# Block means of v from pair sums: three averaging products per batch instead of six

## The chip, the cores and the metric

The kernel runs on one core of one Trainium2 chip. Its time is the device time of one launch in microseconds (us), the median of 3 runs: 488.06 us, with runs from 487.51 to 488.13 us. Engines are named as in the profile: PE (TensorE, with PEld for its weight loads), DVE (VectorE), ACT (ScalarE), POOL (GpSimd) and SP (SyncE, which issues all DMAs here; SPq is its queue).

## The reference

Three layers follow each other. The first is an attention of 2 batches, 8 heads, 768 tokens and 64 features per head, in which each token sees the tokens fewer than 16 positions away and, beside them, 24 block summaries (a block is 32 tokens). The second and third are feed-forward layers over the 1536 tokens, 512 wide. Only this part of the attention touches the change:

```python
k_sum = k.reshape(B, H, nb, block, D).max(axis=3)
v_sum = v.reshape(B, H, nb, block, D).mean(axis=3)        # block = 32, nb = 24
...
v_all = np.concatenate([v, v_sum], axis=2)
return np.matmul(a, v_all)
```

So per batch 24 rows of 512 values are wanted, each the mean of 32 neighbouring rows of v.

## The kernel before, in words

Everything is float32. PE takes a float32 product with 128x512 outputs as two passes; the feed-forward products use pairs of a rounded high part and a rest ("hi" and "lo"), three products each (`mm3x`, lines 104 to 106).

**Block means (`sum_v`, line 180 on).** Six DMAs bring 128 tokens each into `v_sb`. For each, one PE product with a slice of the matrix `avg` as stationary operand adds the means of its four blocks to 24 rows of `vs_ps`: `avg` holds 1/32 at row r, column 120 + r // 32, and the slice that starts at column 24 - 4i puts the blocks of the i-th 128 tokens into their rows. ACT copies the 24 rows to `vsum`, and POOL copies them below the windows of v (`vw`, line 97), where the attention's second product (`x_ps`, line 251) reads them. `sum_v(0)` runs at the start, `sum_v(1)` at the first tick of the main loop. The tile of `v_sb` for batch 1 gives its buffer on to `k_sb` of batch 1 (line 168), so that load waits until the products on `v_sb` are done. The four `ksum` maxima of DVE (line 173) read that `k_sb`.

**What runs beside it.** Attention of 64 tokens at a time is cut in three: scores (`s_ps`, line 215; masks on DVE, line 221; exponentials on ACT, line 224; normalising on POOL, line 229), transposes (`p_ps`, line 234, and the copy `pT`, line 236) and the product with v (`x_ps`). Two such pieces give an `xT` tile of 128 tokens, a hi part by ACT (line 135) and a lo part by DVE (line 101), which the products `h` with `w_in` read. The weights arrive as 64-bit words and are converted: ACT line 122, POOL line 125, DVE lines 126, 127 and 131, then ACT line 135 for hi and DVE line 101 for lo. Eight such conversions, of `w_in`, run in the first 50 us.

**Who sets the order.** Through the first two layers the program's own order holds on SP (a manual schedule), so every DMA stands where the code issues it. On the other engines a scheduler that times the program in advance orders the instructions; an edit at one place can therefore move instructions far from it. (In the later part of the third layer PE's order is the program's own too.) Each engine runs its list strictly in that order.

Of the kernel before, what the change touches and what calls it, by code (L numbers as in the profile page):

```python
# [15 lines left out]
ALU = mybir.AluOpType  # L16
# [3 lines left out]
B, H, S, D = 2, 8, 768, 64  # L20
BLOCK, WINDOW = 32, 16
NB = S // BLOCK
# [4 lines left out]
PAD = 16  # L27
NP = H // 2
DM, F1, F2 = 512, 1024, 2048
# [22 lines left out]
def tile_kernel(ctx: ExitStack, tc: tile.TileContext, qd, kT, v, w_in, w_out, g_ln, w_in2, w_out2,  # L52
                ident_d, mask_d, avg_d, out):
    nc = tc.nc
# [38 lines left out]
    avg = p_at.tile([128, 128 + NB], F32, name="avg", bufs=1)  # L93
# [84 lines left out]
    def sum_v(b):  # L178
        pst = psb.tile([128, DM], F32, tag="b", name="vs_ps")
        v_sb = p_k.tile([128, NP, S + 2 * PAD], F32, tag="k", name="v_sb", bufs=2).rearrange("p a s -> p (a s)")  # L180
        for i in range(S // 128):
            vt = v_sb[:, i * DM:(i + 1) * DM]
            nc.sync.dma_start(vt, v[b, PAD + i * 128:PAD + (i + 1) * 128, :])
            c0 = NB - i * 4
            nc.tensor.matmul(pst, lhsT=avg[:, c0:c0 + 128], rhs=vt, start=i == 0, stop=i == S // 128 - 1)
        vsum[b] = p_at.tile([128, DM], F32, tag="vsum", name="vsum", bufs=1)
        nc.scalar.activation(vsum[b][WIN:KW, :], pst[WIN:KW, :], AF.Copy)

# [14 lines left out]
    def attn_s(n):  # L203
        b, t = divmod(n, NT)
        j, half = divmod(n, 2)
        kw = kws[n % NKW]
        if n not in q_bd:
            load_q(n)
        if t < NKW and n:
            copy_pool(kw[:, :, WIN:KW], ksum[b])  # L210
        if n < NCOPY:
            copy_pool(kw[:, :, 0:WIN], k_sb[b][:, :, t * TQ:t * TQ + WIN])
        sps = psb.tile([128, NP, 128], F32, tag="b", name="s_ps")
        for p in range(NP):
            nc.tensor.matmul(sps[:, p, 0:KW], lhsT=q_bd[n][:, p, :], rhs=kw[:, p, :], start=True, stop=True)  # L215
        sm = p_at.tile([128, NP, KW], F32, tag="sm", name="sm", bufs=NBUF)
        st = p_at.tile([128, 4, NP], F32, tag="st", name="st", bufs=NBUF)
        nm, ss, ri = (st[:, i, :] for i in range(3))
        mi = 1 if t == 0 else (2 if t == NT - 1 else 0)
        for p in range(NP):  # L220
            nc.vector.tensor_tensor_reduce(sm[:, p, :], sps[:, p, 0:KW], mask[:, mi, :], -scale, 3.0e38,  # L221
                                           op0=ALU.add, op1=ALU.min, accum_out=nm[:, p:p + 1])
        for p in range(NP):
            nc.scalar.activation(sm[:, p, :], sm[:, p, :], AF.Exp, bias=nm[:, p:p + 1], scale=-1.0,  # L224
                                 accum_out=ss[:, p:p + 1])
        nc.vector.tensor_scalar(ri, ss, 1e-9, None, op0=ALU.add)
        nc.vector.reciprocal(ri, ri)  # L227
        for p in range(NP):
            nc.gpsimd.tensor_scalar(sm[:, p, :], sm[:, p, :], ri[:, p:p + 1], 1.0, op0=ALU.mult, op1=ALU.mult)  # L229
        live[n] = sm  # L230
# [209 lines left out]
    def more(n=1):  # L440
        for _ in range(n):
            if conv:
                conv.pop(0)()
# [23 lines left out]
    nc.sync.dma_start(ident, ident_d)  # L467
    load_q(0)
    more()
    nc.sync.dma_start(avg, avg_d)  # L470
    attn_s(0)
    more()
    attn_s(1)
    sum_v(0)
    more(2)
    attn_p(0)
# [29 lines left out]
    for t, (j, n) in enumerate(ticks):  # L506
        s_n, p_n, x_n = t + LEAD, t + LEAD - 2, t + LEAD - 3
        if t == 0:
            sum_v(1)
        elif t == 1:  # L510
            load_k(1)
        elif t == 3:
            sum_k(1)
# [263 lines left out]
```

## Time and profile before

| | us |
|---|---|
| median of 3 runs (lowest, highest) | 488.06 (487.51, 488.13) |
| the profiled execution | 489.18 |
| its span | 487.4 |
| PE busy | 461.4 (95%) |
| DVE busy | 330.6 (68%) |
| ACT busy | 284.2 (58%) |
| POOL busy | 120.2 (25%) |

The profile is of one execution, whose time is the span and 1.78 us around it. A share of the span is a mean over parts with different limits: in the first 12 us PE does nothing, and in the last 37 us DVE next to nothing. The chain that ended last lies 71% on PE and 14% on DVE. "Idle before" and "waited for" are inferred from semaphores. The ends of PE's products are modelled, so that PE reads as busy where its next product already stands in line.

### The profile page before, as it was taken

To read this page: it belongs to the slowest core of one execution; us is meant where nothing else is said; L and a number is where in the kernel's file an instruction comes from. 1 tells how busy PE (TensorE), PEld (TensorE's weight loads), DVE (VectorE), ACT (ScalarE), POOL (GpSimd) and SP (SyncE) were. 2 spreads that over 40 slices of the span, in tenths; PEclk is the share of its full clock that TensorE was granted. 3 is DMA by queue.
4 is the path that set the end of the run, shared out by engine and by line. 5 is a ranking of instruction groups with operands and counts; after the bars stand their busy time and mean duration, and the time that the engine had idled before them with its cause. 6 is when DMAs were issued, how large, how long until landed. Compare 5 with 4: busy or idle time off the path is not lost.

```text
span 487.4 us, 7395 instructions
## 1 busy us (share of the span) xinstructions
PE 461.4 (95%) x2568; PEld 389.2 (80%) x2568; DVE 330.6 (68%) x747; ACT 284.2 (58%) x623; POOL 120.2 (25%) x198
## 2 busy tenths in 40 slices
PE   0989999899998999999999999999999999999996
PEld 0666688689997998899888778888888888888885
DVE  3699869988489377969898999567665565541000
ACT  1675788786568347654864757457676666660001
POOL 2797375475425221312212200000000000000000
PEclk9989999999999999999999999999999999999999
DMA  8994668555253413397679754551112212278112
GB/s 280 359 349 153 181 183 287 173 172 180 68 165 121 150 60 103 110 327 242 210 245 305 270 194 152 184 205 44 64 67 87 86 44 86 94 303 292 47 43 86
DMA packets 40117, 82.47 MB, mean 169 GB/s; under 512 B 9616, under 2 KB 18448, under 8 KB 40080
## 3 DMA queue, kind: packets, MB, share of 16 engines
q1 hardware_dynamic: 40080, 82.00, 50.5%
q8 instruction: 20, 0.33, 0.3%
q14 instruction: 17, 0.14, 0.1%
HBM read 70.46 MB, written 11.53 MB: 168 GB/s over the span
## 4 chain that ended last, share of the span: by engine, by line
PE 71%; DVE 14%; DMA 6%; ACT 3%; issue 3%; POOL 2%; SPq 0%; ACTq 0%; DVEq 0%; POOLq 0%
PE o_ps L106 8%; PE o_ps L104 7%; PE o_ps L105 7%; PE c L104 5%; PE c L105 5%; PE c L106 5%; PE h L106 5%; PE h L104 5%; PE h L105 5%; PE y_ps L104 4%; PE y_ps L106 4%; PE y_ps L105 4%; PE s_ps L215 3%; DVE conv L127 2%; ACT sm L224 2%
## 5 line engine op out<-in xcount | busy, mean ns | idle before, releaser
L125 POOL TENSOR_SCALAR conv<-conv 128x512 f32<-128x512 f32 x48 | 38.0, 792 | 93.4 <-ACT conv L122 91.3
L229 POOL TENSOR_SCALAR sm<-sm,st 128x120 f32<-128x120 f32 x96 | 47.1, 508 | 30.8 <-DVE st L227 26.3
L104 PE MATMUL o_ps<-w4r,g_hl 128*128 128x512 f32 x128 | 49.9, 390 | 0.3 <-ACT g_hl L135 0.3
L105 PE MATMUL o_ps<-w4r,g_hl 128*128 128x512 f32 x128 | 49.8, 389 | 0.0
L106 PE MATMUL o_ps<-w4r,g_hl 128*128 128x512 f32 x128 | 45.5, 391 | 0.2 <-DVE g_hl L101 0.2
L104 PE MATMUL y_ps<-lnT,w_out 128*128 128x384 f32 x128 | 43.7, 341 | 1.1 <-DVE lnT L101 1.0
L105 PE MATMUL y_ps<-lnT,w_out 128*128 128x384 f32 x128 | 43.2, 337 | 0.0
L106 PE MATMUL y_ps<-lnT,w_out 128*128 128x384 f32 x128 | 43.0, 337 | 0.0
L104 PE MATMUL h<-w_in,xT 128*128 128x512 f32 x96 | 39.9, 415 | 2.5 <-ACT xT L135 2.5
L215 PE MATMUL s_ps<-kw,q_bd 128*128 128x120 f32 x192 | 28.1, 295 | 13.3 <-POOL kw L97 12.1
L224 ACT ACTIVATE sm<-sm,st 128x120 f32<-128x120 f32 x96 | 36.8, 389 | 5.2 <-DVE st L221 5.2
L106 PE MATMUL h<-w_in,xT 128*128 128x512 f32 x96 | 38.7, 403 | 0.7 <-DVE xT L101 0.7
L215 PEld LDWEIGHTS s_ps<-kw,q_bd 128*128 128x128 f32 x192 | 26.1, 207 | 15.4 <-POOL kw L97 12.1
L105 PE MATMUL h<-w_in,xT 128*128 128x512 f32 x96 | 38.1, 397 | 0.0
L612 DVE COPY y<-o_ps 128x512 f32<-128x512 f32 x5 | 3.4, 690 | 42.9 <-PE o_ps L106 42.9
L584 ACT ACTIVATE y<-y 128x512 f32<-128x512 f32 x48 | 30.0, 627 | 0.8
L614 ACT ACTIVATE y<-o_ps 128x512 f32<-128x512 f32 x6 | 3.6, 598 | 43.9 <-PE o_ps L106 43.9
L104 PEld LDWEIGHTS o_ps<-w4r,g_hl 128*128 128x128 f32 x128 | 24.0, 188 | 5.7 <-ACT g_hl L135 0.7
L106 PEld LDWEIGHTS o_ps<-w4r,g_hl 128*128 128x128 f32 x128 | 23.8, 188 | 5.9 <-DVE g_hl L101 1.1
L122 ACT ACTIVATE conv<-y 128x512 f32<-128x512 f32 x30 | 20.0, 670 | 14.4 <-DMA y<-in_w_in 12.8
L105 PEld LDWEIGHTS o_ps<-w4r,g_hl 128*128 128x128 f32 x128 | 24.1, 188 | 5.0
L101 DVE TENSOR_TENSOR g_hl<-y,g_hl 128x512 fp32r<-128x512 f32 x32 | 22.1, 692 | 8.2 <-ACT g_hl L135 7.9
(146 smaller groups left out, 1254.4 us busy)
## 6 DMA issues: line engine op xcount, KB each, us to landing
w4r<-w4d SPq DMA_DIRECT2D x38, 512.0 KB, 3.8
y<-in_w_in SPq DMA_DIRECT2D x16, 512.0 KB, 5.5
w4d<-w3f SPq DMA_DIRECT2D x16, 512.0 KB, 3.1
y<-in_w_out SPq DMA_DIRECT2D x14, 512.0 KB, 5.4
q_bd<-in_qd SPq DMA_DIRECT2D x24, 256.0 KB, 5.8
bits<-in_w_out SPq DMA_DIRECT2D x10, 512.0 KB, 5.4
w4l<-w4d SPq DMA_DIRECT2D x10, 512.0 KB, 4.2
vw<-in_v SPq DMA_DIRECT2D x24, 192.0 KB, 4.1
```

Of the source, the lines that this page charges most:

```text
L101: nc.vector.tensor_tensor(out_, x, hi.bitcast(F32), op=ALU.subtract)
L104: nc.tensor.matmul(ps, lhsT=l[0][ls], rhs=r[0][rs], start=first, stop=False, skip_group_check=parts)
L105: nc.tensor.matmul(ps, lhsT=l[0][ls], rhs=r[1][rs], start=False, stop=False, skip_group_check=parts)
L106: nc.tensor.matmul(ps, lhsT=l[1][ls], rhs=r[0][rs], start=False, stop=last, skip_group_check=parts)
L122: first = nc.scalar.activation(x, high.bitcast(F32), AF.Abs)
L125: nc.gpsimd.tensor_scalar(x, x, F64_HUGE, F64_TINY, op0=ALU.min, op1=ALU.max)
L127: nc.vector.scalar_tensor_tensor(a, high, -0x40000000, a, op0=ALU.bitwise_and, op1=ALU.bitwise_or)
L215: nc.tensor.matmul(sps[:, p, 0:KW], lhsT=q_bd[n][:, p, :], rhs=kw[:, p, :], start=True, stop=True)
L224: nc.scalar.activation(sm[:, p, :], sm[:, p, :], AF.Exp, bias=nm[:, p:p + 1], scale=-1.0, accum_out=ss[:, p:p + 1])
L229: nc.gpsimd.tensor_scalar(sm[:, p, :], sm[:, p, :], ri[:, p:p + 1], 1.0, op0=ALU.mult, op1=ALU.mult)
L584: nc.scalar.activation(m, m, AF.Exp, scale=-1.0)
L614: nc.scalar.activation(o, ops[t], AF.Copy)
```

## The change

A batch's v is loaded by three DMAs of 256 tokens; a partition receives two neighbouring tokens side by side. DVE adds the second to the first, and one product per DMA averages the sums, three in place of six. A sum of two tokens has its block at row r // 16, so `avg` has to hold 1/32 at column 120 + r // 16. The array in memory stays as it was; two DMAs of 64 rows each fetch its rows in another order: blocks of 16 rows (every second block of 16) fill 64 partitions, the second time shifted by 4 columns. The second leaves columns 0 to 3 of its 64 partitions unwritten; the slices that the products read begin at columns 24, 16 and 8.

```diff
-        for i in range(S // 128):
-            vt = v_sb[:, i * DM:(i + 1) * DM]
-            nc.sync.dma_start(vt, v[b, PAD + i * 128:PAD + (i + 1) * 128, :])
-            c0 = NB - i * 4
-            nc.tensor.matmul(pst, lhsT=avg[:, c0:c0 + 128], rhs=vt, start=i == 0, stop=i == S // 128 - 1)
+        for i in range(S // 256):
+            vt = v_sb[:, i * 2 * DM:(i + 1) * 2 * DM].rearrange("p (r f) -> p r f", r=2)
+            nc.sync.dma_start(vt, v[b, PAD + i * 256:PAD + (i + 1) * 256, :].rearrange("(p r) f -> p r f", r=2))
+            nc.vector.tensor_tensor(vt[:, 0], vt[:, 0], vt[:, 1], op=ALU.add)
+            c0 = NB - i * 8
+            nc.tensor.matmul(pst, lhsT=avg[:, c0:c0 + 128], rhs=vt[:, 0], start=i == 0, stop=i == S // 256 - 1)
...
-    nc.sync.dma_start(avg, avg_d)
+    for h in range(2):
+        nc.sync.dma_start(avg[h * 64:(h + 1) * 64, h * 4:], avg_d.rearrange("(c h p) k -> c h p k", h=2, p=16)[
+            :, 0, :, :128 + NB - h * 4])
```

The scheduler orders PE, DVE, ACT and POOL anew, up to the middle of the second layer. Line numbers behind line 185 grow by one in the changed kernel (226 becomes 227, 227 becomes 228), those behind line 470 by three. Two places on DVE are shown.

First, DVE's list after the masks of the first two pieces, while the first two weight tiles are converted (`conv`, `w_in`) and their softmax sums inverted (`st`). Before:

```order
L126 TENSOR_SCALAR conv<-conv 128x512
L227 RECIPROCAL st<-st 128x4
L127 SCALAR_TENSOR_TENSOR conv<-y_65,conv 128x512
L131 SCALAR_TENSOR_TENSOR conv<-y_65,conv 128x512
L226 TENSOR_SCALAR st<-st 128x4
L227 RECIPROCAL st<-st 128x4
L126 TENSOR_SCALAR conv<-conv 128x512
L101 TENSOR_TENSOR w_in_90<-conv,w_in_89 128x512
L127 SCALAR_TENSOR_TENSOR conv<-y_65,conv 128x512
L131 SCALAR_TENSOR_TENSOR conv<-y_65,conv 128x512
L101 TENSOR_TENSOR w_in_90<-conv,w_in_89 128x512
L126 TENSOR_SCALAR conv<-conv 128x512
```

The same place in the changed kernel:

```order
L126 TENSOR_SCALAR conv<-conv 128x512
L184 TENSOR_TENSOR v_sb<-v_sb 128x512
L228 RECIPROCAL st<-st 128x4
L127 SCALAR_TENSOR_TENSOR conv<-y_65,conv 128x512
L227 TENSOR_SCALAR st<-st 128x4
L184 TENSOR_TENSOR v_sb<-v_sb 128x512
L131 SCALAR_TENSOR_TENSOR conv<-y_65,conv 128x512
L228 RECIPROCAL st<-st 128x4
L126 TENSOR_SCALAR conv<-conv 128x512
L184 TENSOR_TENSOR v_sb<-v_sb 128x512
L127 SCALAR_TENSOR_TENSOR conv<-y_65,conv 128x512
L101 TENSOR_TENSOR w_in_90<-conv,w_in_89 128x512
```

The three additions of batch 0 (L184) stand between the steps of the first two conversions, the first of them ahead of the reciprocal on which POOL's normalising waits.

Second, DVE's list around the lo part of the second `xT` tile (tokens 128 to 255), at the end of the eighth conversion. Before:

```order
L101 TENSOR_TENSOR w_in_90<-conv,w_in_89 128x512
L173 TENSOR_REDUCE ksum<-k_sb 128x24 x2
L226 TENSOR_SCALAR st<-st 128x4
L221 ISA sm,st<-s_ps,mask 128x120
L221 ISA st 128x1
L221 ISA sm,st<-s_ps,mask 128x120
L221 ISA st 128x1
L101 TENSOR_TENSOR xT<-x_ps,xT 128x512
```

The same place in the changed kernel:

```order
L131 SCALAR_TENSOR_TENSOR conv<-y_65,conv 128x512
L227 TENSOR_SCALAR st<-st 128x4
L173 TENSOR_REDUCE ksum<-k_sb 128x24
L228 RECIPROCAL st<-st 128x4
L101 TENSOR_TENSOR xT<-x_ps,xT 128x512
L101 TENSOR_TENSOR w_in_90<-conv,w_in_89 128x512
L173 TENSOR_REDUCE ksum<-k_sb 128x24
```

The `xT` part has moved ahead of the eighth conversion's lo part, of one maximum and of two masks; one maximum still stands ahead of it.

## Rows read from the trace of the kernel before

**Rows 1.** Busy time by stretch: stretch, length, busy us (instructions) per engine, clock, DMA.
```profile
24.00:36.00 12.00, 9.82 (x78) 8.31 (x78) 11.61 (x41) 9.35 (x34) 11.25 (x17) 0.86 0.98 347
36.00:48.00 12.00, 11.45 (x82) 7.60 (x82) 10.94 (x34) 6.74 (x21) 9.95 (x15) 1.00 0.47 153
48.00:60.00 12.00, 11.28 (x87) 9.06 (x86) 10.66 (x33) 8.42 (x27) 3.87 (x11) 1.00 0.63 179
300.00:350.00 50.00, 50.00 (x222) 41.40 (x221) 33.89 (x47) 33.97 (x56) 0.00 (x0) 1.00 0.35 120
```

**Rows 2.** Chain that ended last, in order of time: start us, us, what.
```profile
40.67 0.68 DVE conv L127
41.44 0.93 DVE w_in L101
47.79 1.72 DVE ksum L173 x2
49.98 0.61 DVE xT L101
50.64 0.50 PE h L106
```

**Rows 3.** Timeline of PE: start us, us, engine, line, [idle before <- releaser].
```profile
39.77 2.74 PE L185 MATMUL vs_ps<-v_sb,avg 128*128 128x512 f32 x6
50.64 0.50 PE L106 MATMUL h<-w_in,xT 128*128 128x512 f32 x1 [0.72 <-DVE xT L101]
```

**Rows 4.** Tile vs_ps: duration ns min/median/max, first and last start.
```profile
L185 PE MATMUL vs_ps<-v_sb,avg x24: 592/592/1064, 15.6 to 41.9; 128*128 128x512 f32 x24
```

**Rows 5.** Line 101 from 12 to 52 us: duration ns min/median/max.
```profile
L101 DVE TENSOR_TENSOR w_in<-conv,w_in x8: 692/740/1006, 19.7 to 47.1; 128x512 fp32r<-128x512 f32 x8
```

**Rows 6.** Groups of DVE by form, 12 to 52 us: busy us, mean ns, idle before.
```profile
L221 DVE CUSTOM_DVE_ANT_0 sm<-s_ps,mask 128x120 f32<-128x120 f32 x32 | 7.1, 274 | 4.9 <-PE s_ps L215 4.8
L127 DVE SCALAR_TENSOR_TENSOR conv<-y,conv 128x512 int32<-128x512 int32 x8 | 6.5, 817 | 0.1
L101 DVE TENSOR_TENSOR w_in<-conv,w_in 128x512 fp32r<-128x512 f32 x8 | 6.4, 796 | 1.6 <-ACT w_in L135 1.4
L131 DVE SCALAR_TENSOR_TENSOR conv<-y,conv 128x512 int32<-128x512 int32 x8 | 6.1, 763 | 0.1
L126 DVE TENSOR_SCALAR conv<-conv 128x512 int32<-128x512 int32 x8 | 3.7, 465 | 1.0 <-POOL conv L125 1.0
L173 DVE TENSOR_REDUCE ksum<-k_sb 128x24 f32<-128x768 f32 x4 | 3.7, 933 | 0.0
```

**Rows 7.** Timeline of DVE, its holes between 20 and 50 us.
```profile
22.38 0.75 DVE L101 TENSOR_TENSOR w_in<-conv,w_in 128x512 fp32r<-128x512 f32 x1 [0.70 <-ACT w_in L135]
24.09 0.43 DVE L126 TENSOR_SCALAR conv<-conv 128x512 int32<-128x512 int32 x1 [0.96 <-POOL conv L125]
...
43.67 0.69 DVE L101 TENSOR_TENSOR w_in<-conv,w_in 128x512 fp32r<-128x512 f32 x1 [0.70 <-ACT w_in L135]
```

**Rows 8.** Clock: busy time by stretch, columns as in rows 1.
```profile
28.00:30.00 2.00, 0.80 (x3) 0.44 (x4) 1.93 (x7) 2.00 (x10) 2.00 (x4) 1.00 0.86 255
30.00:32.00 2.00, 2.00 (x11) 1.99 (x11) 1.87 (x6) 1.34 (x3) 1.92 (x4) 0.54 0.90 303
```

**Rows 9.** Load of k_sb for batch 1, SP's timeline; tile k_sb, issue to landing.
```profile
42.54 1.75 SPq L168 DMA_DIRECT2D k_sb<-in_kT  x4
...
DMA to landing us min/median/max: 2.9/4.7/7.1
```

**Rows 10.** DMA, 0 to 45 us: packets, MB, share of 16 engines; issue, KB, landing.
```profile
q1 hardware_dynamic: 5771, 12.62, 82.7%
...
avg<-in_avg SPq DMA_DIRECT2D x1, 76.0 KB, 5.6
```

**Rows 11.** Timelines of PE's weight loads and of DVE, 16 to 17 us.
```profile
16.53 0.19 PEld L185 LDWEIGHTS vs_ps<-v_sb,avg 128*128 128x128 f32 x1 [0.50 <-DMA v_sb<-in_v]
16.76 0.42 DVE L126 TENSOR_SCALAR conv<-conv 128x512 int32<-128x512 int32 x1
```

## The prediction

> **What bounds the kernel now.** The page's first line is read first, and it misleads: PE is busy for 95% of the span, and the change takes work from PE. So the table by stretch comes next [rows 1]. From 300 us on PE is busy without a gap, and what the first layers lose or win reaches the end whole. The block means lie ahead of 44 us, and there DVE is as full as PE: 11.61 of 12 us in 24 to 36 against PE's 9.82, 10.94 against 11.45 in 36 to 48. Which of the two others wait for is read from the chain in order of time [rows 2]: in the forties its pieces are the weight conversions on DVE, then two maxima, then the lo part of the second `xT` tile at 49.98; PE comes into the chain only behind that, at 50.64. PE's timeline says the same from its side: the product at 50.64 waited 0.72 us for that `xT` part [rows 3]. So to 50.6 us the bound is DVE's list, and the question is when the second `xT` is through; PE's 12 products per weight half stand behind it. From there PE bounds the rest with few holes.
>
> **What is removed.** Of 12 averaging products 6 go. One is two passes (24 records for 12 products [rows 4]); six passes took 2.74 us, the last with its full 0.592 us [rows 3, 4], so the pitch is (2.74 - 0.592) / 5 = 0.43 us, a product is 0.86 us, and 6 of them are 5.2 us of PE, 2.6 per batch. They ran while PE waited for transposed softmax (batch 0) or for weights and `xT` (batch 1). Since PE's next bounded piece starts on DVE's word, I value these 5.2 us at nothing. Their cover is DVE's list ahead of 50.6 us; were it shorter, up to 5.2 us would be won.
>
> **What is added on DVE.** Six additions of two float32 operands of 128x512. The nearest row is line 101 of the conversions, with the same shape and two operands: 0.69 us at the least, 0.74 median, 1.01 at the most beside POOL's work [rows 5]. I take 0.74: 6 x 0.74 = 4.4 us, from 4.1 to 6.1.
>
> **What is moved.** The scheduler has re-sorted DVE's list, and what counts is the set that stands ahead of the second `xT` part. Comparing the two lists, three things left it: the eighth conversion's lo part, one maximum, and two of the four masks of the eighth piece. By their rows [rows 5, 6] that is 0.74 + 0.93 + 2 x 0.27 = 2.2 us. So the list ahead of it grows by 4.4 - 2.2 = 2.2 us. Against that stand DVE's holes on this stretch: 0.70 us and 0.96 us ahead of 24.1 and 0.70 us ahead of 43.7 [rows 7]. The first two lie behind the additions of batch 0. They end on ACT's and POOL's work, which the additions do not lengthen much: POOL's eight normalisings start one addition later at the most, and the wait of 0.96 us is for POOL's conversion step behind them. So I take 1.66 us as filled. The third ends on ACT's hi part, which follows DVE's own step; I take half of it, 0.3. In all 2.0 us, from 1.3 to 2.4.
>
> **What is late next.** Three things were moved behind the second `xT` part: the eighth lo part, which the middle product of the last weight slice reads, one maximum, and two masks. PE's new list has products of the second tile between, so I cost that at nothing; its cover is the 24 products that begin at 50 us, and without them it is the lo part's 0.74 us.
>
> **The loads.** Bytes are the same; SP issues 3 loads of v for 6 and 2 of `avg` for 1, so what is queued behind them comes two places earlier at the start and three at batch 1. I cost that at nothing: in the first 45 us the 16 DMA engines are busy for 82.7% [rows 10], so bytes set the landings, not issues.
>
> **The clock.** PE's granted clock fell to 0.54 in 30 to 32 us, near the lower of its two levels (1.2 GHz, against 2.4), after a stretch in which PE was busy for 0.80 of 2 us [rows 8]. With three products fewer before it, that may begin earlier. I cost it at nothing: DVE's list covers PE there until 50.6 us. Without that cover, the first tile's 12 products would take twice their time at the full clock, which is 50.00 us / 222 = 0.225 us each [rows 1]: 2.7 us more.
>
> **The sum.** +2.2 - 2.0 = +0.2 us at the second `xT` and, with PE bounding the rest, at the end. The profiled execution took 489.18 us for a span of 487.40 (1.78 us around it), so one like it would take 489.4. The median shown is 488.06, 1.12 us under the profiled execution, and the sum is the same on top of it: 488.3 us. Within this case the additions at 0.69 to 1.01 us and the holes at 1.3 to 2.4 us give 4.1 - 2.2 - 2.4 = -0.5 to 6.1 - 2.2 - 1.3 = +2.6, or 487.6 to 490.7; the upper end needs every addition at the longest, so I take 487.5 to 489.8 as its own range. What a measurement can tell from no change is 0.2%, 1.0 us: 487.1 to 489.0 counts as the same.
>
> **Rivals.**
>
> *PE was the bound after all (faster).* PE's list mixes averaging products with weight products, scores and transposes, and if the masks and the second `xT` wait for those, all of it moves up. For it: PE is busy for 11.45 of 12 us in 36 to 48 [rows 1]. Against it: in this stretch the chain has no PE piece before 50.64 [rows 2]. If one batch's share is won, 2.6 us: 485.5 us; if both, 482.9. Chance 0.30.
>
> *The load of k behind the third sum (slower).* One maximum still stands ahead of the second `xT` part, and it reads the `k_sb` of batch 1, whose load waits until the averaging products have left the buffer: before, they ended at 39.77 + 2.74 = 42.5 and the load was issued at 42.54 [rows 3, 9]. Now the last product waits for DVE's sixth addition. From that addition to the maximum DVE has two lots of four masks (8 x 0.27), two lo parts (1.6), two steps of line 131 (1.5), one of 127 (0.8) and one of 126 (0.5): 6.6 us [rows 6]. The load's way is the product's 0.86, the issue and 4.7 us to land, some 5.8; the longest landing is 7.1 [rows 9]. It decides from a landing of 5.7 us on: then DVE stands still with the `xT` part queued behind, at the longest landing for 7.1 - 5.7 = 1.4 us: 488.3 + 1.4 = 489.7 us. For it: the slack is 1.0 us, and DVE's steps overlap a little, which shortens it. Against it: that load ran in a queue nearly empty at 42 us (DMA share 0.47 in 36 to 48 [rows 1]). Chance 0.19.
>
> *The re-sorted `avg` holds the queue up (slower).* Its two loads have a source whose outer step counts only 4 blocks. If only four DMA engines carry them, each gets 32 of the 128 rows in place of 8. A packet cost 0.827 x 45 us x 16 / 5771 = 0.103 us on average [rows 10], so these four are late by 24 x 0.103 = 2.5 us for everything queued behind, v first. Before, the second load of v had landed by 16.53, and PE had waited 0.50 us for it [rows 11]; in the new list the first addition follows at 17.2, behind the step at 16.76 with 0.42. So it would wait up to 16.5 + 2.5 - 17.2 = 1.8 us, with the reciprocals and POOL's normalising queued behind it: 488.3 + 1.8 = 490.1 us. Against it: rows of 608 bytes may cost far less than the mean packet of 2.2 KB, and DVE has two holes behind it. Chance 0.13. The Trainium skill (DMA: Bandwidth & Descriptors, section on why a DMA increments its semaphore by 16) says that a transfer is spread over the largest number of engines, up to 16, that divides the slowest dimension of both its patterns; here these are 64 and 4, which would be four engines. No row of before shows such a transfer, so the rule raises this rival's chance and nothing else.
>
> **How the numbers follow.** The forecast, no change that can be told, has 0.38; the faster rival 0.30, the two slower ones 0.32. Predicted: 488.3 us. The range reaches to the faster rival at one batch's worth and to the slower ones: 485.2 to 490.8 us, which leaves out the full 5.2 us of gain and a pile-up of both slower rivals. Of the forecast's 0.38 the upper end of its range (489.0 to 489.8) takes 0.07 as slower and the lower 0.03 as faster; of each rival 0.02 falls within 1 us of no change: faster 0.31, same 0.34, slower 0.35.
>
> **What would show it.** Right: six additions (line 184) of 0.7 to 1.0 us; the holes ahead of the second weight tile's lo part and of the third conversion's first step gone; the second `xT` lo part starting between 49.4 and 51; PE's wait for it as before, and more idle PE ahead of 50 us by about 5. The second rival shows as DVE idle ahead of its first maximum with `k_sb` as the releaser, the third as DVE idle ahead of the first addition with `v_sb` or PE's first averaging product waiting for `avg`. The first shows as the second `xT` lo part, and PE's products behind it, well ahead of 49 us. The forecast is wrong if the second `xT` stays within 1 us and the end moves by more than 1 us: then the re-sorted lists behind it, which I did not cost, decide.

## The result, and the profile after

| | before | changed |
|---|---|---|
| median of 6 runs, us (lowest, highest) | 487.99 (486.56, 488.44) | 491.86 (490.66, 494.37) |
| ratio (95% interval) | | 1.0093 (1.0073 to 1.0114) |
| the profiled execution, its span, us | 489.18, 487.4 | 491.13, 489.4 |
| PE busy, us | 461.4 | 457.9 |

The changed kernel is slower by 3.9 us; 488.3 was predicted, with a range up to 490.8. The profiled executions differ by 2.0 us only: that of before lies above its kernel's median, that of the changed kernel below. So places are read from traces, sizes from medians.

The table by stretch, columns as in [rows 1], of the changed kernel, and below it the last of these stretches in the kernel before:

```profile
36.00:48.00 12.00, 10.87 (x79) 7.75 (x77) 12.00 (x44) 8.29 (x28) 9.49 (x12) 0.97 0.44 154
72.00:84.00 12.00, 9.92 (x83) 8.23 (x82) 10.96 (x30) 10.25 (x29) 5.21 (x10) 1.00 0.88 269
```

```profile
72.00:84.00 12.00, 11.63 (x92) 9.67 (x91) 11.71 (x31) 10.11 (x25) 6.87 (x13) 1.00 0.83 261
```

DVE has no hole left in 36 to 48 us (12.00 of 12, before 10.94). The new thing is the last stretch: PE does 9.92 us of work in 72 to 84, where the kernel before did 11.63. The lo parts of the second and the fifth `xT` on DVE, in the kernel before (start, duration, line):

```profile
49.91 0.68 DVE L101 TENSOR_TENSOR xT<-x_ps,xT 128x512 fp32r<-128x512 f32 x1
...
80.08 0.68 DVE L101 TENSOR_TENSOR xT<-x_ps,xT 128x512 fp32r<-128x512 f32 x1
```

DVE's timeline of the changed kernel around the same two places:

```profile
47.39 0.68 DVE L101 TENSOR_TENSOR w_in<-conv,w_in 128x512 fp32r<-128x512 f32 x1
...
49.85 0.65 DVE L101 TENSOR_TENSOR xT<-x_ps,xT 128x512 fp32r<-128x512 f32 x1
50.42 0.96 DVE L101 TENSOR_TENSOR w_in<-conv,w_in 128x512 fp32r<-128x512 f32 x1
...
80.54 0.74 DVE L147 SCALAR_TENSOR_TENSOR w_out<-conv,gT,w_out 128x512 fp32r<-128x512 f32 x1
81.20 0.68 DVE L131 SCALAR_TENSOR_TENSOR conv<-y,conv 128x512 int32<-128x512 int32 x1
81.80 1.21 DVE L280 SCALAR_TENSOR_TENSOR ln<-h,ln 128x1024 f32<-128x1024 f32 x1
...
83.08 0.68 DVE L101 TENSOR_TENSOR xT<-x_ps,xT 128x512 fp32r<-128x512 f32 x1
```

The second `xT` lo part begins at 49.85 us, 0.06 earlier than before. That is no finer than a trace can tell: e8 and e16 below, with the kernel before's work and order up to there, have it at 48.51 and 48.84, and e6, with the changed kernel's, at 50.45. But the third begins at 62.69, 1.7 later than its 60.97 of before, and the fifth at 83.08, 3.0 later than 80.08: three long steps now stand ahead of it. PE's timeline of the changed kernel shows the two waits that answer to the one of [rows 3]:

```profile
48.12 0.50 PE L105 MATMUL h<-w_in,xT 128*128 128x512 f32 x1 [1.25 <-DVE w_in L101]
...
83.81 0.66 PE L297 MATMUL t_ps<-ident,ln 128*128 128x128 f32 x4 [1.58 <-DVE xT L101]
```

The wait of 0.72 us for the second `xT` is gone. PE waits for the seventh lo part of `w_in` instead, and later for the fifth `xT` to free a PSUM buffer (PSUM is where PE's products land; its buffers are handed on). The chain in order of time (start, us, what) shows where PE stood in line at the first place:

```profile
46.79 0.59 ACT vsum L188
...
47.41 0.87 ACT sm L225 x4
...
48.32 0.66 POOL sm L230
...
49.02 0.33 PE p_ps L235
...
55.60 0.45 PE h L105 x2
56.05 0.24 PE h L106
...
56.32 1.24 DVE st L277
```

Where [rows 2] had DVE conversions and one wait of PE, the chain now goes through ACT's copy of the means, ACT's exponentials and POOL. The first tile's last products run at 55.6, behind those of the second tile, so its layer norm (line 277) begins at 56.32; before, the same maximum began at 52.70.

DVE's hole that answers to the middle one of [rows 7] was to be filled. It has grown, from 0.96 to 2.00 us: POOL, whose conversion step ends it, first had its eight normalisings, which waited 0.73 us for the reciprocal behind the first addition and took 6.11 us for 5.61. The other two holes of [rows 7] are gone. The load of [rows 9] goes out 2.4 us later (timelines of DVE, of POOL and of SP's queue):

```profile
24.56 0.83 DVE L126 TENSOR_SCALAR conv<-conv 128x512 int32<-128x512 int32 x1 [2.00 <-POOL conv L125]
```

```profile
17.72 6.11 POOL L230 TENSOR_SCALAR sm<-sm,st 128x120 f32<-128x120 f32 x8 [0.73 <-DVE st L228]
```

```profile
44.92 1.75 SPq L168 DMA_DIRECT2D k_sb<-in_kT  x4
```

The low clock of [rows 8] comes some 3 us later, where DVE is as full as before (2.00 and 1.97 of 2 us):

```profile
32.00:34.00 2.00, 0.82 (x2) 0.56 (x3) 2.00 (x12) 2.00 (x8) 1.83 (x4) 0.84 0.78 252
34.00:36.00 2.00, 2.00 (x11) 1.95 (x10) 1.97 (x5) 1.20 (x5) 1.39 (x3) 0.50 0.97 360
```

The additions are about as costed, 5.0 us in all for 4.4 (duration ns min/median/max, first and last start):

```profile
L184 DVE TENSOR_TENSOR v_sb<-v_sb x6: 673/772/1098, 16.4 to 42.9; 128x512 f32<-128x512 f32 x6
```

### The profile page after: what moved, and what is told of

It reads as the page before. It is cut to its first block, busy times and chain, and to the rows that moved or that the text cites. A ratio compares the mean times of both kernels' runs of the same rounds, so it can differ in the third digit from the quotient of the medians.

```text
span 489.4 us, 7368 instructions
## 1 busy us (share of the span) xinstructions
PE 457.9 (94%) x2556; PEld 388.8 (79%) x2556; DVE 335.5 (69%) x753; ACT 284.4 (58%) x623; POOL 122.7 (25%) x198
## 4 chain that ended last, share of the span: by engine, by line
PE 81%; DVE 7%; DMA 4%; ACT 3%; issue 2%; SPq 1%; POOL 1%; DVEq 0%; ACTq 0%
PE o_ps L106 9%; PE o_ps L105 9%; PE o_ps L104 9%; PE h L104 6%; PE h L106 6%; PE h L105 6%; PE c L106 5%; PE c L105 5%; PE c L104 5%; PE y_ps L104 4%; PE y_ps L106 4%; PE y_ps L105 4%; PE s_ps L216 3%; DMA q_bd<-in_qd 3%; PE x_ps L252 2%
## 5 line engine op out<-in xcount | busy, mean ns | idle before, releaser
L125 POOL TENSOR_SCALAR conv<-conv 128x512 f32<-128x512 f32 x48 | 36.8, 767 | 90.2 <-ACT conv L122 89.2
L230 POOL TENSOR_SCALAR sm<-sm,st 128x120 f32<-128x120 f32 x96 | 49.5, 533 | 24.4 <-DVE st L228 11.2
L216 PEld LDWEIGHTS s_ps<-kw,q_bd 128*128 128x128 f32 x192 | 27.3, 213 | 16.8 <-POOL kw L97 11.4
L222 DVE CUSTOM_DVE_ANT_0 sm<-s_ps,mask 128x120 f32<-128x120 f32 x96 | 21.3, 275 | 10.6 <-PE s_ps L216 9.8
```

What stands on the lines that cost most here:

```text
L125: nc.gpsimd.tensor_scalar(x, x, F64_HUGE, F64_TINY, op0=ALU.min, op1=ALU.max)
```

## The experiments

Where an order is laid down, each instruction of PE, DVE, ACT and POOL is chained behind the one that a list names, without a semaphore:

```diff
+        for a, b in zip(numbers, numbers[1:]):
+            tc.add_manual_dep(mine[b], mine[a].name, NoSync, reason="order by list")
```

The lists are those that the scheduler made for the kernel before ("old order") and for the changed one ("new order"). All is against the kernel before, timed on the same chip in the same rounds: the ratio with its interval, and the difference of the medians in us (the two are worked out apart and differ by up to 0.9 us, in e9).

### Work and order, apart

The edit of e1 is the list alone: old order under the changed kernel. e2 is the reverse. e3 takes the additions out of the changed kernel, e4 puts its two `avg` loads into the kernel before (its means are of other tokens):

```diff
 e3
-            nc.vector.tensor_tensor(vt[:, 0], vt[:, 0], vt[:, 1], op=ALU.add)
 e4
-    nc.sync.dma_start(avg, avg_d)
+    for h in range(2):
+        nc.sync.dma_start(avg[h * 64:(h + 1) * 64, h * 4:], avg_d.rearrange(...)[:, 0, :, :128 + NB - h * 4])
```

> The changed kernel's instructions (six additions, six products), but PE, DVE, ACT and POOL follow the order of the kernel before; each addition stands behind the same DVE instruction as in the changed kernel. Theory W (the additions' 4.4 us on DVE's full list are what is lost): slower than before by 3 to 5 us, 491 to 493. Theory S (the re-sorted lists behind 50 us are what is lost): within 1 us of before, 487 to 489; a little faster if PE's 5.2 us count.

Measured: 490.20 us, 1.0056 (1.0038 to 1.0075), +3.0 us.

> The kernel before (12 products, no addition), but PE, DVE, ACT and POOL follow the order of the changed kernel; two products stand where one of the changed kernel does. Theory S: as slow as the changed kernel, 490 to 493. Theory W: within 1 us of before, 487 to 489.

Measured: 491.62 us, 1.0093 (1.0068 to 1.0117), +4.5 us.

> The changed kernel in its own order without the six additions: the products read the first token of each pair alone, so the means leave out every second token. Theory W: 4 us faster than the changed kernel, at most 488. Theory S: under 1.5 us faster than it, 490 to 492.

Measured: 488.97 us, 1.0031 (1.0013 to 1.0048), +1.8 us.

> The kernel before in its own order, with avg fetched by the changed kernel's two re-sorted loads, so that the block means are of the wrong rows. Theories W and S: within 0.5 us of before. Third rival of the prediction (the two loads sit on few DMA engines): up to 1.8 us slower, with the first product waiting for avg or v until 17 us or later.

Measured: 487.95 us, 1.0004 (0.9985 to 1.0022), +0.8 us.

The loads of `avg` cost nothing that can be told. Neither theory stands alone: new work in the old order is slower, and so is old work in the new order. The two do not add up either (3.0 and 4.5 against 3.9); each order was made for its own work, which may be why. DVE's `xT` lo parts of e1 (second and fifth):

```profile
52.26 0.68 DVE L101 TENSOR_TENSOR xT<-x_ps,xT 128x512 fp32r<-128x512 f32 x1
...
82.40 0.68 DVE L101 TENSOR_TENSOR xT<-x_ps,xT 128x512 fp32r<-128x512 f32 x1
```

In the old order the second is 2.35 us later than the 49.91 of before, and the fifth still 2.32 later than 80.08: the delay is carried whole, and the end has it (+3.0). The holes of [rows 7] were hardly filled: in e1 they are still 0.70, 0.51 and 0.70 us (before 0.70, 0.96, 0.70):

```profile
24.36 0.75 DVE L101 TENSOR_TENSOR w_in<-conv,w_in 128x512 fp32r<-128x512 f32 x1 [0.70 <-ACT w_in L135]
25.62 0.43 DVE L126 TENSOR_SCALAR conv<-conv 128x512 int32<-128x512 int32 x1 [0.51 <-POOL conv L125]
...
45.39 0.69 DVE L101 TENSOR_TENSOR w_in<-conv,w_in 128x512 fp32r<-128x512 f32 x1 [0.70 <-ACT w_in L135]
```

### Products alone, one move, and the order in two halves

e5 is e3's work in the old order. e6 moves one instruction of the changed kernel's DVE list; e7 and e8 give the kernel before the new order up to 57 us or from 57 us on:

```diff
 e6, DVE
+83.08  line 101, lo part of the fifth xT
 80.54  line 147, lo part of w_out
 81.20  line 131, conversion
 81.80  line 280, layer norm
-83.08  line 101, lo part of the fifth xT
```

> The kernel before's order on PE, DVE, ACT and POOL, with the three products per batch and the two loads of avg, but without the six additions (it leaves out every second token of the means). Against the kernel before: theory 'PE's products were free' (as the prediction had it, the six products taken away are covered by DVE's list): 0, from -0.6 to +0.6 us. Rival 'they were worth something': within the new order, six products more cost 2.65 us (491.62 against 488.97), so -2.6 us here too. Against new work in old order (+2.7 to +3.0 us) the difference is the price of the additions in the old order: 2.7 to 3 by the first, 5.3 to 5.6 by the second.

Measured: 489.17 us, 1.0026 (1.0004 to 1.0047), +1.4 us.

> The changed kernel with its own order, one DVE instruction moved: the lo part of the fifth xT (at 83.08 us) stands ahead of lines 147, 131 and 280 (80.54 us on), where the kernel before had it. Theory 'the late order costs': PE's wait of 1.58 us at 83.81 for a PSUM buffer goes, and the time falls by 1 to 1.6 us against the changed kernel, to +2.5 to +3 us over the kernel before. Rival 'made up later anyway': within 0.5 us of the changed kernel's +3.9 to +4.5 us.

Measured: 490.97 us, 1.0062 (1.0042 to 1.0082), +3.2 us.

> The kernel before's work (twelve products, no additions) in the new order up to about 57 us (to the scores of the next piece on PE, the first layer-norm maximum on DVE) and in the old order behind. The whole new order costs this work +4.45 us. Theory 'late' (the cost lies behind 57 us): 0 to +1 us over the kernel before. Theory 'early': +3.5 to +4.5. By the starts of x_ps in the profiled executions (+2.9 us at the third, +4.4 at the eighth) a split, +2 to +3, would not surprise.

Measured: 493.14 us, 1.0109 (1.0071 to 1.0146), +5.4 us.

> The other half: the kernel before's work in the old order up to about 57 us and the new order behind. Theory 'late': +3.5 to +4.5 us over the kernel before. Theory 'early': 0 to +1. If the halves add up, this and the run before it sum to 4.45.

Measured: 488.83 us, 1.0014 (0.9994 to 1.0035), +1.0 us.

e6 came near to what the late theory had: moved ahead, the fifth lo part begins at 81.14, the wait for the buffer is gone, and the kernel stands where e1 stands (1.0062, 1.0056). The halves missed: for the old work the first half of the new order costs as much as the whole or more (5.4 against 4.5 us), and the second hardly anything, although e8 has the late fifth lo part, and PE's wait for it, as the changed kernel has them:

```profile
81.12 0.66 PE L296 MATMUL t_ps<-ident,ln 128*128 128x128 f32 x4 [1.59 <-DVE xT L101]
```

One early piece shows in e7 (and in e2, with 1.40 us): DVE waits for the load of k of batch 1, the prediction's second rival.

```profile
50.92 0.95 DVE L173 TENSOR_REDUCE ksum<-k_sb 128x24 f32<-128x768 f32 x1 [1.22 <-DMA k_sb<-in_kT]
```

e7 is no clean half, though. The first tile's end comes late in it, as in the new order, and the old list behind it does not allow for that: PE waits 1.64 us at 63.4 for a small layer-norm step of DVE (line 283). e5 missed both theories: six products less and no additions, and still slower. In the profiled execution the clock shows where. The table by stretch, columns as in [rows 1], of the kernel before and then of e5:

```profile
92.00:94.00 2.00, 1.51 (x13) 1.40 (x13) 2.00 (x9) 2.00 (x7) 0.45 (x1) 1.00 0.98 297
94.00:96.00 2.00, 1.58 (x8) 0.72 (x7) 2.00 (x11) 2.00 (x9) 1.47 (x4) 1.00 0.88 264
96.00:98.00 2.00, 2.00 (x14) 1.82 (x14) 1.65 (x8) 2.00 (x9) 1.10 (x2) 1.00 1.01 323
```

```profile
92.00:94.00 2.00, 1.90 (x13) 1.78 (x14) 2.00 (x7) 2.00 (x5) 0.07 (x1) 0.82 0.92 261
94.00:96.00 2.00, 1.79 (x6) 0.82 (x5) 2.00 (x12) 2.00 (x11) 1.47 (x4) 0.50 0.82 265
96.00:98.00 2.00, 1.67 (x8) 1.70 (x9) 1.36 (x6) 2.00 (x9) 1.48 (x3) 0.50 1.03 348
98.00:100.00 2.00, 2.00 (x7) 1.61 (x7) 0.35 (x2) 1.10 (x5) 1.92 (x5) 0.50 0.97 307
```

In both, PE has just waited 1.76 us for POOL. PE's timelines, of the kernel before and of e5:

```profile
92.49 0.62 PE L234 MATMUL p_ps<-ident,sm 128*120 128x128 f32 x4 [1.76 <-POOL conv L125]
```

```profile
92.11 0.62 PE L234 MATMUL p_ps<-ident,sm 128*120 128x128 f32 x4 [1.76 <-POOL conv L125]
```

In e5 the clock then falls from the upper to the lower of its two levels (0.50 is 1.2 of 2.4 GHz) and is back by 102 us. What it costs stands in the `x_ps` products on either side, of the kernel before and of e5:

```profile
89.57 1.15 PE L251 MATMUL x_ps<-pT,vw 120*64 120x64 f32 x32
...
102.15 1.15 PE L251 MATMUL x_ps<-pT,vw 120*64 120x64 f32 x32
```

```profile
89.19 1.15 PE L251 MATMUL x_ps<-pT,vw 120*64 120x64 f32 x32
...
104.32 1.15 PE L251 MATMUL x_ps<-pT,vw 120*64 120x64 f32 x32
```

e5 enters 0.38 us ahead and leaves 2.17 behind. The missing products need not be the reason: e4, with all twelve, falls to the lower level behind the same wait, at 92.00, and has 13.12 us between the two `x_ps` (the kernel before 12.58, e5 15.13):

```profile
92.00:94.00 2.00, 2.00 (x10) 2.00 (x11) 2.00 (x7) 2.00 (x4) 0.00 (x0) 0.51 0.96 269
```

The timed executions of e5 point the same way. The five with a mean granted clock of 0.993 took 487.68 to 489.78 us, the two of the kernel before with it 488.46 and 489.36; the one at 0.996 took 487.77, thirteen of the kernel before 486.59 to 488.76. At the same clock no difference can be told.

### The seventh and eighth lo part, and a tick later

e9 moves, in the changed kernel, the eighth lo part (50.42) ahead of the second `xT` and the two last products of the first tile ahead of the second tile's; e10 does this and the move of e6. e11 and e12 let the program issue batch 1's means later, in the changed kernel and in the one before:

```diff
-        if t == 0:
+        if t == 1:
             sum_v(1)
-        elif t == 1:
+        elif t == 2:
             load_k(1)
-        elif t == 3:
+        elif t == 4:
             sum_k(1)
```

> The changed kernel with its own order, but for the eighth lo part of w_in (DVE, 50.42 us) ahead of the second xT lo part, and PE's two products of the first tile that read it and follow it (55.4 us on) ahead of the second tile's, as in the kernel before. Theory 'the end of the first tile': this is what the early order costs; DVE's first layer-norm maximum begins near 52.5 us instead of 56.32, and the time falls by 1 to 2.5 us against the changed kernel (+3.9 to +4.5 us over the kernel before), to +2 to +3. Rival 'another early piece, or the additions': the maximum moves but the time stays within 0.7 us of the changed kernel's.

Measured: 492.60 us, 1.0086 (1.0062 to 1.0111), +5.1 us.

> The run before it and the lo part of the fifth xT moved ahead (alone +3.0 us over the kernel before, 1.5 less than the changed kernel). If both theories hold and add up: +0.5 to +1.5 us over the kernel before. If only the second move counts: about +3.

Measured: 490.51 us, 1.0058 (1.0041 to 1.0075), +3.0 us.

> The changed kernel with batch 1's means, its load of k and its maxima one tick later in the program (ticks 1, 2 and 4 for 0, 1 and 3); the scheduler sets the order. Theory 'DVE's list to the second xT is the bound and each instruction on it counts': three additions are still ahead of it (its list is 80 long instead of 85) but the maxima are not; 1 to 3 us under the changed kernel. Theory 'what the scheduler makes of the list decides': anything from -2 to +2 us of the changed kernel, with the sign set by where the first layer-norm maximum begins (56.32 us there, 52.70 in the kernel before).

Measured: 500.33 us, 1.0262 (1.0242 to 1.0281), +12.8 us.

> The same edit of ticks on the kernel before, without the change. It tells what a re-sorting by itself is worth: the same two theories; by the first -1 to -2 us against the kernel before (eight instructions fewer ahead of the second xT, 74 for 82), by the second within 2 us either way.

Measured: 497.15 us, 1.0192 (1.0172 to 1.0212), +9.7 us.

The eighth lo part was no loss: the first tile's maximum moved up only to 55.48 (two maxima of `ksum` ahead of it waited 0.38 and 0.49 us for the load of k), and the time not at all. The move of e6 pays again: e10 stands 0.28% under e9. Both theories missed e11 and e12, and e12 is the run that judges my whole way of reckoning. Its second and third `xT` lo parts, and DVE's hole between:

```profile
43.72 0.66 DVE L101 TENSOR_TENSOR xT<-x_ps,xT 128x512 fp32r<-128x512 f32 x1
...
56.42 0.28 DVE L221 CUSTOM_DVE_ANT_0 sm<-s_ps,mask 128x120 f32<-128x120 f32 x1 [8.20 <-PE s_ps L215]
...
65.75 0.68 DVE L101 TENSOR_TENSOR xT<-x_ps,xT 128x512 fp32r<-128x512 f32 x1
```

The second `xT` is 6.2 us earlier than before and the end 9.7 us later. PE, with batch 1's products and a whole tile's products in front of the next scores, had become the bound in 48 to 60 us, and DVE stood still for 8.20.

### Loads, batches, and the late lo part by itself

e13 keeps the change's loads but averages both halves of a loaded tile on PE; e14 and e15 add on DVE for batch 0 or batch 1 alone. All three are in the old order:

```diff
-            nc.vector.tensor_tensor(vt[:, 0], vt[:, 0], vt[:, 1], op=ALU.add)
+            parts = 2                    # e14: 1 if b == 0 else 2;  e15: 1 if b == 1 else 2
+            if parts == 1:
+                nc.vector.tensor_tensor(vt[:, 0], vt[:, 0], vt[:, 1], op=ALU.add)
-            nc.tensor.matmul(pst, lhsT=avg[:, c0:c0 + 128], rhs=vt[:, 0], ...)
+            for r in range(parts):
+                nc.tensor.matmul(pst, lhsT=avg[:, c0:c0 + 128], rhs=vt[:, r], ...)
```

e16 is the kernel before, with the fifth `xT` lo part and two lo parts of `lnT` behind lines 279 and 281 on DVE.

> The kernel before's order and twelve products, with the change's loads (three of 256 tokens per batch, two of avg) and no additions: each half of a loaded tile is averaged by its own product. Taking products away in the old order made it 1.4 us slower (e5), not faster. Theory 'PE idles and its clock falls': with twelve products back this run stands at the kernel before, -0.5 to +0.5 us. Rival 'the larger loads land later' (PE waited 1.1 us for v there): +1 to +1.8 us, as e5.

Measured: 487.96 us, 1.0002 (0.9992 to 1.0011), +0.2 us.

> Old order and new loads; three additions and three products for batch 0, six products and no additions for batch 1. New work in old order costs +2.7 to +3.0 us with both batches. Theory 'batch 1's additions pay, batch 0's fall into DVE's holes': 0 to +0.7 us over the twelve-product run of this job. Rival 'each addition pays alike': +1.0 to +1.5.

Measured: 489.62 us, 1.0037 (1.0024 to 1.0050), +1.9 us.

> The mirror: six products for batch 0, three additions and three products for batch 1. First theory: +1.5 to +2.5 us over the twelve-product run of this job; rival: +1.0 to +1.5.

Measured: 490.59 us, 1.0063 (1.0044 to 1.0081), +2.8 us.

> The kernel before with one piece of its DVE list changed: the fifth xT's lo part and two lo parts of lnT stand behind lines 279 and 281, as the changed kernel has them (there PE waits 1.58 us for it, and moving it back gave 1.5 us). Theory 'this place costs by itself': +1 to +1.6 us over the kernel before, with PE's wait for the PSUM buffer near 82 us. Rival 'only on top of the other delays': within 0.5 us.

Measured: 493.49 us, 1.0123 (1.0105 to 1.0141), +5.7 us.

The loads cost nothing that can be told, so e5's loss is not theirs. Batch 0's additions cost too, where I had put DVE's holes: both theories on the batches missed. The medians of the two batches do not add up to e1 (+3.0), but the traces nearly do: the second `xT` lo part begins at 49.32 in e13, 50.62 in e14, 51.26 in e15 and 52.26 in e1, which is 1.30, 1.94 and 2.94 us later.

The late lo part of e16 costs far more than its expectation. In the old order line 279 waits for ACT, and the lo part now waits behind it. DVE's timeline of e16, PE's, and its clock behind it:

```profile
81.14 1.23 DVE L279 SCALAR_TENSOR_TENSOR ln<-h,ln 128x1024 f32<-128x1024 f32 x1 [1.41 <-ACT ln L278]
```

```profile
83.09 0.66 PE L296 MATMUL t_ps<-ident,ln 128*128 128x128 f32 x4 [3.33 <-DVE xT L101]
```

```profile
82.00:84.00 2.00, 0.91 (x6) 0.87 (x7) 2.00 (x6) 0.21 (x1) 0.00 (x0) 1.00 1.07 384
84.00:86.00 2.00, 2.00 (x6) 1.51 (x6) 1.67 (x4) 2.00 (x4) 0.62 (x1) 0.55 0.56 166
86.00:88.00 2.00, 2.00 (x7) 1.58 (x6) 0.50 (x2) 0.09 (x1) 0.66 (x1) 0.59 0.02 8
```

After the wait of 3.33 us, PE works without a gap for 4 us with the clock near its lower level: (1 - 0.55) x 2 + (1 - 0.59) x 2 = 1.7 us of work not done, beside the wait itself.

### The wait at 48 us

Two runs on the changed kernel move DVE's seventh lo part (47.39) ahead of the four masks at 45.91; e18 adds the move of e6:

```diff
 DVE
+47.39  line 101, seventh lo part of w_in
 45.91  line 222, four masks
 46.72  line 227
 46.79  line 127, conversion
-47.39  line 101, seventh lo part of w_in
```

> The changed kernel with its own order, one DVE instruction moved: the seventh lo part of w_in (47.39 us), for which PE waited 1.25 us at 48.12, stands ahead of the four masks at 45.91. Theory 'PE, not only DVE, was late at 50 us, for want of this lo part': PE's wait shrinks to 0.3 us or less, the third x_ps (58.00 us) begins about 1 us earlier, and the time falls by 0.8 to 1.2 us, to about +3 us over the kernel before. Rival 'another wait takes its place': within 0.5 us of the changed kernel's +3.9 to +4.5.

Measured: 492.16 us, 1.0099 (1.0074 to 1.0124), +4.5 us.

> Both DVE moves that took a wait away: the seventh lo part of w_in and the lo part of the fifth xT (alone +3.0 us over the kernel before). If the two waits are the cost of the re-sorting and add up: +1.5 to +2 us. If the first is covered by another wait: about +3.

Measured: 491.41 us, 1.0073 (1.0054 to 1.0091), +3.8 us.

The rival holds. PE's timeline of e17:

```profile
49.81 0.32 PE L235 MATMUL p_ps<-ident,sm 128*120 128x128 f32 x1 [0.92 <-POOL sm L230]
```

The wait for the lo part is gone, and PE waits for POOL's normalising in its place. The masks had moved back, and ACT's exponentials and POOL stand behind them. The move of e6 pays once more: e18 stands 0.26% under e17.

## Why the prediction was wrong

**The milestone held, the inference from it was wrong.** The second `xT` (the milestone) was put 0.2 us later and came 0.06 earlier, the same within what traces of one order differ by there (1.4 us). The step that failed is "The sum": "+2.2 - 2.0 = +0.2 us at the second `xT` and, with PE bounding the rest, at the end". From the second to the fifth `xT` the changed kernel lost 3.0 us: the re-sorted lists behind 50 us, which the prediction had at nothing and named in its last sign of being wrong, are where the end is decided. e12 shows that the milestone does not decide: 6.2 us earlier there, 9.7 later at the end. Behind 50 us PE is not a bound with few holes in any order, but in the one that it had.

**"What is moved" was a debt, not a saving.** I took 2.2 us off because a lo part, a maximum and masks went behind the second `xT`. Left in the old order, the additions make the second `xT` 2.35 us late (e1), where 4.4 - 2.0 gives 2.4. That agreement is luck: the additions took 4.7 us there, and of the three holes 0.45 us was filled, not 2.0; against e13 and e5, in the same order and with the same loads, the second `xT` is 2.94 and 3.61 us late. In the changed kernel the three holes are 2.00 us in all for 2.36, so the 2.0 was wrong there too: POOL's work, which ends the middle one, did start later and take longer. The re-sorting hid the delay at 50 us, and the time was lost later. The kernel in its own order is no better than in the old one, but worse (1.0093 against 1.0056), and one move takes that back (e6, 1.0062).

**"What is late next" looked at the wrong lo part.** The eighth, which I named and costed at nothing, did cost nothing (e9). The seventh, not named, made PE wait 1.25 us at 48.12, but POOL's softmax was as late (e17). The one late piece that runs show to cost lies 33 us behind the part of the list that I compared: the fifth `xT` lo part behind three long steps. Putting it back gives 1.0062 for 1.0093, and again 1.0058 for 1.0086 (e10) and 1.0073 for 1.0099 (e18): a third of the loss. Delaying it in the kernel before costs 5.7 us (e16), but with a wait of PE twice as long; the wait of the changed kernel, in the old work (e8), goes with +1.0 us at the end, which its interval does not tell from nothing.

**"What is removed", valued at nothing.** That PE's 5.2 us were no gain is right (e5, e13 against the first rival). But without them the kernel was 1.4 us slower, and the whole interval of e5 lies above 1. The clock, costed at nothing for the stretch near 31 us, fell near 94 us, far from the change: 2.5 us between two `x_ps` of the profiled e5. Over the timed executions the mean granted clock was 0.992 for e5 and 0.995 for the kernel before beside it, and at the same clock no difference between the two can be told. Why e5 gets the lower clock more often is not shown.

**Rivals.** PE as the bound is out for the old order (e5 is not faster); in the new order six products more do cost, 491.62 against 488.97 us (e2, e3), but the kernel before did not have that order. The load of k came in time in the changed kernel: DVE's first maximum, at 48.90, waited for no load. With little more delay it would not have: the same maximum waited 0.38 us in e9, 1.22 in e7 and 1.40 in e2. The re-sorted `avg` is out (e4, e13). There I weighed the Trainium skill's rule (DMA: Bandwidth & Descriptors, on why a DMA increments its semaphore by 16). How many engines carried these loads no run here shows; the runs show no price for them, at most 0.0011 of the time by e13's interval.

**What adds up, and what stays open.** In sequence, by the ratios: products away 0.26% (e5), additions on top 0.30% (e1), the new order on top 0.37%, of which the one move of e6 takes 0.31% back. Each interval reaches 0.2% to either side, so that a single step is uncertain by about 1 us, nearly as much as it is worth; only the sum, 0.93%, is well clear of that, and the move of e6, seen three times. The steps also depend on their sequence: in the new order the additions cost 0.62% (e3, then the changed kernel), and since e5's time holds more of the low clock than e1's (mean 0.996), the 0.30% is likely too little. With e13 in place of e5, whose clock did not fall, the change's work in the old order costs 0.54% (e1), and with the 0.31% of e6's move that is 0.85 of the 0.93%. Open: what made e5's clock fall more often, where the 1.7 us between the second and the third `xT` are lost (no run moved ACT's copy of the means by itself, which stands in the chain there), and what else beside the load of k the early part of the new order costs old work (e7). No run here beats the kernel before.

## What to carry to other kernels

A milestone that stands still proves nothing when a scheduler re-sorts the list: what left the list ahead of it has to be found behind it, and followed until an engine is idle again. Compare the two orders to the end, and for each long step ask which result now stands behind it that frees a buffer or starts another engine. Work taken from an engine that only waits longer for it need not be worth anything: e5 took 5.2 us from PE and was not faster. And a sum that comes out right at a milestone is no proof of its terms: look at each one in the trace.

## What was not expected of the hardware

The same wait of PE for POOL, 1.76 us near 92 to 99 us, stands in nine profiled kernels. It was followed by the upper clock level in three of them (the kernel before, e13, e14) and by the lower one in six (e1, e4, e5, e7, e15, e16), among them e4, which differs from the kernel before only in two small loads some 80 us earlier. Between the `x_ps` on either side lay 12.6 to 12.8 us in the three, 13.0 to 13.3 in five of the six, and 15.1 in e5, where the lower level lasted until about 100 us. So a wait's price is not its length alone: behind the same 1.76 us it was nothing, some 0.5 us, or 2.5 us more, and behind the 3.33 us of e16 about 1.7.
